# x by tokens on row halves of the array, a batch in one run

## The chip, the cores and the metric

The kernel runs on one core of a Trainium2 chip. The metric is the device time of one execution in microseconds; the median over three runs is 315.53 us (315.52 to 315.60).

## The reference, cut to what matters

```python
# attention without softmax: 8 batches, 8 heads, 576 tokens, head_dim 64
kv = einsum('bhsd,bhse->bhde', k, v)          # 64 x 64 for each head
o = einsum('bhsd,bhde->bhse', q, kv)
x = o / sqrt(mean(o * o, axis=-1) + 1e-6) * g_norm
# the heads side by side: x is 4608 tokens x 512
a = x @ w_a; b = x @ w_b                      # d_ff = 1536
out = (a * b) @ w_out                         # 4608 x 512
```

## The kernel before, in words

The matmuls run in bf16 with fp32 sums in PSUM, which is one tile `P` of 8 banks of 512 columns. The 4608 tokens are taken in 9 strips of 512 (`STRIP`). A strip of the feed-forward part has 12 units (`Unit`, one for each 128 columns of d_ff): group a is 4 matmuls with `w_a` as weights (`part_a`), which ScalarE casts into `asb` (L335); group b is 4 with `w_b` (`part_b`), which VectorE multiplies by `asb` into `ab` (L339). After the units come four groups of 12 matmuls with `w_out` (`ffn_o`, L156), each copied out by ScalarE or VectorE in turn and stored through the SP queue.

Batches 0 and 1 of the attention part are worked at the start, by head. Batches 2 to 7 are worked by token, one batch in each of the strips 1 to 6, in between the units: batch `b = s + 1` in strip `s`, whose x the next strips read from `xt`. The order is written out by hand: `slot(A, s, n)` is called after unit or output group n, and with n - 0.5 between its two halves, and it issues the piece that is due at that n.

A batch by token goes like this. `kv` forms k^T v of each pair of heads, as 40 matmuls on the two column halves of the array (L173), into bank 7; in strips 3 and 5 it is done for two batches. `kv_out` copies the results into `kvb`, one 128 x 128 block for each pair of heads, whose off-diagonal quarters are zero (L184). Then x comes in five chunks of 128 tokens (576 tokens: the fifth starts at 448 and uses only its last 64). For chunk c, `tx` runs 4 matmuls, one for each pair of heads, with 128 tokens of q^T as weights (128 rows: two heads of 64) and the block of `kvb` streamed (128 columns), into bank 5 + c % 3 (L271), and ScalarE squares it (L278). A half step later `tss` sums by head on VectorE (L282), another half later `trs` takes the reciprocal root on ScalarE (L287) and GpSimd multiplies it with g (L294), and 1.5 steps after that `txt` multiplies on VectorE (L303) and issues a DMA transpose into `xt` on the SP queue (L305).

The groups of the units take their banks from `ab_bank()`, which goes round 4, 1, 2, 0; output groups take bank 3 (`O`) or a bank of that round in turn. So banks 0 to 4 belong to the feed-forward part and 5 to 7 to the attention part.

```python
AB = (4, 1, 2, 0)
n_ab = [0]
def ab_bank():
    n_ab[0] += 1
    return AB[(n_ab[0] - 1) % len(AB)]
```

q, k and v of batches 2 to 7 are loaded by DMAs that GpSimd issues (`load_late`); it first waits, in a copy of one element (`gate`, L136), for an earlier q^T. `transpose_q` brings q^T by a DMA transpose on the SP queue.

Of the kernel before, what the change touches and what calls it, by code (L numbers as in the profile page):

```python
# [8 lines left out]
FP32 = mybir.dt.float32  # L9
BF16 = mybir.dt.bfloat16  # L10
AF = mybir.ActivationFunctionType
# [4 lines left out]
def kernel(  # L16
# [11 lines left out]
    nc = tc.nc  # L28

    B, H, S, D = q.shape  # L30
    d_model = H * D
# [4 lines left out]
    NP = H // 2  # L36
    HF = S // 2
    STRIP = 512
# [10 lines left out]
    def sb(shape, dt, name):  # L49
        return pool.tile(shape, dt, name=name, tag=name)  # L50
# [11 lines left out]
    LC = S // 128  # L62
# [4 lines left out]
    qT = [sb([128, NP, S], BF16, f"qT{i}") for i in range(2)]  # L67
    kvs = [sb([128, NP, D], BF16, f"kvs{i}") for i in range(2)]

    kvb = [sb([128, NP, 128], BF16, f"kvb{i}") for i in range(2)]  # L70
    xt = sb([128, KC, n_tok], BF16, "xt")
    abt = [[sb([128, STRIP], BF16, f"ab{i}_{f}") for f in range(FC)] for i in range(2)]
    a_sb = [sb([128, STRIP], BF16, f"asb{i}") for i in range(4)]
# [1 line left out]
    rs = [sb([128, 2, HF], FP32, f"rs{i}") for i in range(3)]  # L75

    k_x = sb([128, 2 * EC * D], FP32, "k_x")
    k32 = k_x[0:EP].rearrange("p (h c d) -> p h c d", h=2, c=EC)

    sqt = [sb([128, H, D], FP32, f"sqt{i}") for i in range(2)]  # L80
    sqt.append(k_x[:, 0 : H * D].rearrange("p (h d) -> p h d", h=H))
    sst = [sb([128, H], FP32, f"sst{i}") for i in range(3)]
    rst = [sb([128, H], FP32, f"rst{i}") for i in range(3)]
    g_all = sb([128, D], FP32, "g_all")
    o_sb = [sb([128, d_model], FP32, f"osb{i}") for i in range(4)]
    o_end = sb([128, d_model // 2], FP32, "o_end")
# [18 lines left out]
    P = psum.tile([128, 8, STRIP], FP32, name="P", tag="P")  # L105
    O = 3
# [47 lines left out]
    def product(o, lhsT, rhs, halves=False, **kw):  # L154
        for r in (slice(0, D), slice(D, 2 * D)) if halves else (slice(0, 2 * D),):
            nc.tensor.matmul(o[r], lhsT=lhsT[:, r], rhs=rhs, **kw)  # L156


    class Attn:
# [18 lines left out]
                        stop=(c == len(rows) - 1),  # L178
                    )

        def kv_out(self, ps, src, copy=nc.scalar.copy):
            for j in range(2):
                r = slice(j * D, (j + 1) * D)
                copy(kvb[self.b % 2][r, ps, r], src[r])  # L184


        def kv1(self, p, i):
# [60 lines left out]
        def x(self, p, i0, halves=False):  # L248
            for h in range(2):
                product(  # L250
                    P[:, i0 + h, 0:HF],
                    kvb[self.b % 2][:, p, :],
                    self.qT[:, p, h * HF : (h + 1) * HF],
                    halves,
                    start=True,
                    stop=True,
                )
# [4 lines left out]
            t0 = min(c * 128, S - 128)  # L262
            return t0, slice(c * 128 - t0, 128)

        def by_head(self, i):
            return P[:, i, :].rearrange("t (h d) -> t h d", h=H)

        def tx(self, c, i):
            t0, r = self.rows(c)
            for p in range(NP):  # L270
                nc.tensor.matmul(  # L271
                    P[:, i, p * 128 : (p + 1) * 128],
                    lhsT=self.qT[:, p, t0 : t0 + 128],
                    rhs=kvb[self.b % 2][:, p, :],
                    start=True,
                    stop=True,
                )
            nc.scalar.activation(sqt[c % 3][r], self.by_head(i)[r], AF.Square)  # L278

        def tss(self, c):  # L280
            _, r = self.rows(c)
            nc.vector.reduce_sum(sst[c % 3][r], sqt[c % 3][r], axis=mybir.AxisListType.X)  # L282

        def trs(self, c):
            _, r = self.rows(c)
            n = r.stop - r.start
            nc.scalar.activation(  # L287
                rst[c % 3][r],
                sst[c % 3][r],
                AF.Abs_reciprocal_sqrt,  # L290
                bias=eps_t[r],
                scale=1.0 / D,
            )
            nc.gpsimd.tensor_mul(  # L294
                sqt[c % 3][r],
                rst[c % 3][r].unsqueeze(2).to_broadcast([n, H, D]),
                g_all[r].unsqueeze(1).to_broadcast([n, H, D]),
            )

        def txt(self, c, i):  # L300
            t0, r = self.rows(c)
            t = x_tok[c // 3][:, c % 3]
            nc.vector.tensor_mul(t[r], self.by_head(i)[r], sqt[c % 3][r])  # L303
            t0 += self.b * S
            nc.sync.dma_start_transpose(  # L305
                xt[:, :, t0 + r.start : t0 + 128], t[r].rearrange("t h d -> t (h d)")
            )


    class Unit:  # L310
        n = 0
# [30 lines left out]
            self.part_a(kcs)  # L342
            self.part_b(kcs)

    AB = (4, 1, 2, 0)
    n_ab = [0]

    def ab_bank():
        n_ab[0] += 1
        return AB[(n_ab[0] - 1) % len(AB)]  # L350

    def ffn_ab(s, fc, between=None):
        u = Unit(s, fc, ab_bank(), ab_bank())
        u.part_a()
        if between:
            between()
        u.part_b()
# [69 lines left out]
    make_identity(nc, ident, nomemset=True)  # L427
    nc.scalar.activation(warm, eps_t, AF.Abs_reciprocal_sqrt)
    nc.vector.memset(ones, 0.0)
    for t in kvb:  # L430
        nc.vector.memset(t, 0.0)
    for t in ktl + vtl:
        nc.vector.memset(t[S - 128 * LC :, :, LC, :], 0.0)
    nc.vector.memset(ones[0:D, 0:D], 1.0 / D)
# [18 lines left out]
    A = Attn(0)  # L453
# [9 lines left out]
    t = P[:, 2, :].bitcast(BF16)[:, 0:S].rearrange("q (c t) -> q c t", c=EC)  # L463
# [4 lines left out]
    for c in range(EC):  # L468
        nc.tensor.matmul(
            P[:, SS, 0 : 2 * D],  # L470
            lhsT=kc0[:, c, :],
            rhs=vc[:, c, :],
            start=(c == 0),
            stop=(c == EC - 1),
        )
    for j in range(2):
        r = slice(j * D, (j + 1) * D)
# [7 lines left out]
    for p in range(1, NP):  # L485
        i = X[p % 2]
# [34 lines left out]
    u3.part_a()  # L521
    u2.part_b()
    u3.part_b()
    n_ab[0] = 0
    for fc in range(4, FC):
        ffn_ab(0, fc)

# [1 line left out]
    A = Attn(1)  # L529
# [27 lines left out]
    u1.first((0, 1, 2))  # L557
    u0.rest((3,))
    u1.rest((3,))
    n_ab[0] = 1  # L560


    def slot(A, s, n):

        kb = P[:, 7, :].rearrange("q (b p e) -> q b p e", b=2, e=D)
        if s == 1:
            k0, xs = 5, (6.5, 8, 9.5, 11, 12.5)
        else:
            k0, x0 = {2: (2, 3.5), 3: (4, 5.5), 4: (0, 1.5), 5: (4, 5.5), 6: (0, 1.5)}[s]
            xs = tuple(x0 + x for x in (0, 1.5, 2.5, 4, 5))  # L570

        if n == k0 and s in (1, 2, 3, 5):
            two = [A] if s < 3 else [A, Attn(s + 2)]
            for i, a in enumerate(two):
                for p in range(NP):
                    a.kv(p, kb[:, i, p, :])
            for i, a in enumerate(two):
                a.kv_out(slice(0, NP), kb[:, i], nc.vector.tensor_copy if i else nc.scalar.copy)
        for c, x in enumerate(xs):
            i = 5 + c % 3  # L580
            if n == x:
                A.tx(c, i)
            elif n == x + 0.5:
                A.tss(c)
            elif n == x + 1:
                A.trs(c)
            elif n == x + 2.5:
                A.txt(c, i)

    for s in range(1, N_STRIP - 1):  # L590
        b = s + 1
        A = Attn(b) if b < B else None
        for n in range(FC + 4):
            amid = (lambda n=n: slot(A, s, n - 0.5)) if A else None
            if n >= FC:
                ffn_o(s, n - FC, ab_bank() if n % 2 else O, amid)
            elif s > 1 or n > 1:
                ffn_ab(s, n, amid)
            if A:
                slot(A, s, n)  # L600

            if s == 1 and n == 3:
                load_late(3)
            if b + 1 < B and n == (12, 4, 8, 5, 8)[s - 1]:
                transpose_q(b + 1)
            if b + 2 < B and n == (14, 10, 14, 8)[s - 1]:
                load_late(b + 2)
# [43 lines left out]
```

## Time and profile before

| what | value |
|---|---|
| median of three runs | 315.53 us |
| the profiled execution's own time | 315.56 us |
| its span, first to last instruction | 313.8 us |
| TensorE's clock granted | 1.00 |
| TensorE busy | 308.6 us, 98% |
| VectorE, ScalarE, GpSimd busy | 141.5, 115.9, 101.2 us |
| matmuls of `tx` (L271) | 120 |
| matmuls of k^T v by token (L173) | 240 of 324 |

The profile is one execution. A matmul's row shows its length from its first to its last effect; matmuls overlap, so the distance of their starts, not the length, is what one costs in a stream. L numbers are lines of the kernel before. Times in the timeline are microseconds from the span's start.

### The profile page before, as it was taken

Reading aid. Unit: us, or ns where it says so; the run is one execution under the profiler, and the core shown is the slowest. Engines: PE = TensorE matmul, PEld = TensorE weight load, DVE = VectorE, ACT = ScalarE, POOL = GpSimd, SP = SyncE. Lnnn points to the kernel's source line nnn. Section 1 sums busy time; section 2 is a strip of 40 time slices with the busy share of each in tenths; the row PEclk is TensorE's granted clock in tenths of the full one; section 3 lists DMA queues with packets and bytes.
Section 4 is the critical chain, followed back from the end, with each engine's and each line's share of the span. In section 5 each row is a group of like instructions: output and inputs, shape, how many; then the busy total and the mean of one; then the engine's idle time right before and its main releaser. Section 6 shows DMA issues by size and latency. Waiting matters only on the chain.

```text
span 313.8 us, 5034 instructions
## 1 busy us (share of the span) xinstructions
PE 308.6 (98%) x1935; PEld 149.0 (47%) x1935; DVE 141.5 (45%) x235; ACT 115.9 (37%) x225; POOL 101.2 (32%) x123
## 2 busy tenths in 40 slices
PE   8999999999999999999999999999999999999995
PEld 3544474454445444544454445544544444444443
DVE  4544335356337703583377123761683134214321
ACT  3643155453246313551464024622651233123310
POOL 8954891282453730139038200320230000000000
PEclk9999999999999999999999999999999999999999
DMA  8999999999799799059988980073022200030002
GB/s 182 197 196 199 201 183 160 229 146 157 172 171 166 103 197 154 2 95 139 207 125 116 169 175 2 17 159 111 1 50 60 102 0 0 36 100 1 0 36 100
DMA packets 94253, 36.19 MB, mean 115 GB/s; under 512 B 64918, under 2 KB 89750, under 8 KB 94230
## 3 DMA queue, kind: packets, MB, share of 16 engines
q0 software_dynamic: 59120, 18.44, 53.8%
q1 hardware_dynamic: 34642, 16.87, 23.3%
q10 hardware_dynamic: 468, 0.57, 0.6%
q8 instruction: 15, 0.25, 0.3%
q14 instruction: 8, 0.07, 0.1%
HBM read 37.78 MB, written 12.98 MB: 162 GB/s over the span
## 4 chain that ended last, share of the span: by engine, by line
PE 86%; DMA 7%; POOL 4%; issue 1%; ACT 0%; POOLq 0%
PE P L321 53%; PE P L156 29%; DMA wb_t<-in_moe_w_b_dram 6%; PE P L271 2%; PE P L173 2%; DMA vt<-in_v_dram 2%; POOL qt L116 1%; POOL wo_t L131 1%; POOL kt L116 1%; POOL vt L116 1%; POOL wa_t L441 0%; POOL wb_t L441 0%; PE P L197 0%; POOL wa_t L127 0%; ACT o_end L619 0%
## 5 line engine op out<-in xcount | busy, mean ns | idle before, releaser
L339 DVE TENSOR_TENSOR ab<-P,asb 128x512 bf16<-128x512 f32 x108 | 74.5, 691 | 103.5 <-PE P L321 87.0
L321 PE MATMUL P<-xt,wa_t 128*128 128x512 bf16 x432 | 111.9, 380 | 0.0
L321 PE MATMUL P<-xt,wb_t 128*128 128x512 bf16 x432 | 111.8, 379 | 0.0
L335 ACT CAST asb<-P 128x512 bf16<-128x512 f32 x108 | 63.0, 585 | 92.4 <-PE P L321 92.4
L156 PE MATMUL P<-wo_t,ab 128*128 128x512 bf16 (+2 forms) x462 | 95.8, 374 | 0.0
L156 PEld LDWEIGHTS <-ab 128*128 128x128 bf16 (+1 forms) x462 | 43.7, 99 | 48.0
L321 PEld LDWEIGHTS <-wa_t 128*128 128x128 bf16 x432 | 41.4, 98 | 47.4 <-issue 0.2
L321 PEld LDWEIGHTS <-wb_t 128*128 128x128 bf16 x432 | 41.5, 98 | 47.0 <-DMA wb_t<-in_moe_w_b_dram 0.2
L294 POOL TENSOR_TENSOR sqt<-rst,g_all 128x512 f32<-128x512 f32 (+1 forms) x24 | 25.0, 1043 | 96.2 <-ACT rst L287 96.2
L392 ACT COPY osb<-P 128x512 f32<-128x512 f32 x17 | 9.9, 585 | 67.5 <-PE P L156 62.2
L394 DVE COPY osb<-P 128x512 f32<-128x512 f32 x18 | 12.4, 691 | 44.0 <-PE P L156 39.5
L139 POOL DMA_DIRECT2D qs<-in_q_dram x12 | 19.8, 1653 | 0.7 <-issue 0.3
L282 DVE TENSOR_REDUCE sst<-sqt 128x8 f32<-128x512 f32 (+1 forms) x24 | 16.3, 680 | 1.9 <-ACT sqt L278 1.4
L303 DVE TENSOR_TENSOR qv<-P,sqt 128x512 bf16<-128x512 f32 (+1 forms) x24 | 16.5, 686 | 0.3
L278 ACT ACTIVATE sqt<-P 128x512 f32<-128x512 f32 (+1 forms) x24 | 14.4, 599 | 4.2 <-PE P L271 4.1
L271 PEld LDWEIGHTS <-qT 128*128 128x128 bf16 x120 | 9.2, 98 | 7.1
L271 PE MATMUL P<-kvb,qT 128*128 128x128 bf16 x120 | 11.6, 220 | 0.0
L287 ACT ACTIVATE rst<-sst,eps_t 128x8 f32<-128x8 f32 (+1 forms) x30 | 9.0, 300 | 4.6 <-DVE sst L282 4.3
L238 DVE SCALAR_TENSOR_TENSOR xt<-P,g_col,rs 128x288 bf16<-128x288 f32 x16 | 7.5, 512 | 5.2 <-ACT rs L228 5.2
L294 POOL TENSOR_TENSOR k_x<-rst,g_all 128x512 f32<-128x512 f32 x6 | 6.3, 1042 | 8.8 <-ACT rst L287 8.8
L131 POOL DMA_DIRECT2D wo_t<-in_moe_w_out_dram x12 | 6.4, 530 | 6.7 <-DMA wb_t<-in_moe_w_b_dram 3.2
L184 ACT CAST kvb<-P 64x64 bf16<-64x64 f32 (+1 forms) x16 | 4.6, 285 | 10.5 <-PE P L173 10.4
(67 smaller groups left out, 123.1 us busy)
## 6 DMA issues: line engine op xcount, KB each, us to landing
out_dram<-osb SPq DMA_DIRECT2D x23, 256.0 KB, 2.1
qs<-in_q_dram POOLq DMA_DIRECT2D x12, 288.0 KB, 6.9
ktl<-in_k_dram POOLq DMA_DIRECT2D x6, 512.0 KB, 8.8
vtl<-in_v_dram POOLq DMA_DIRECT2D x6, 512.0 KB, 11.6
out_dram<-osb SPq DMA_DIRECT2D x13, 128.0 KB, 2.3
wo_t<-in_moe_w_out_dram POOLq DMA_DIRECT2D x12, 128.0 KB, 6.0
wa_t<-in_moe_w_a_dram POOLq DMA_DIRECT2D x5, 256.0 KB, 9.2
wb_t<-in_moe_w_b_dram POOLq DMA_DIRECT2D x5, 256.0 KB, 9.8
```

The source lines that it names most:

```text
L139: nc.gpsimd.dma_start(out=d[:, hs, :], in_=q[b, hs].rearrange("h t d -> t h d"))
L156: nc.tensor.matmul(o[r], lhsT=lhsT[:, r], rhs=rhs, **kw)
L271: nc.tensor.matmul(P[:, i, p * 128 : (p + 1) * 128], lhsT=self.qT[:, p, t0 : t0 + 128], rhs=kvb[self.b % 2][:, p, :], start=True, stop=True,)
L278: nc.scalar.activation(sqt[c % 3][r], self.by_head(i)[r], AF.Square)
L282: nc.vector.reduce_sum(sst[c % 3][r], sqt[c % 3][r], axis=mybir.AxisListType.X)
L294: nc.gpsimd.tensor_mul(sqt[c % 3][r], rst[c % 3][r].unsqueeze(2).to_broadcast([n, H, D]), g_all[r].unsqueeze(1).to_broadcast([n, H, D]),)
L303: nc.vector.tensor_mul(t[r], self.by_head(i)[r], sqt[c % 3][r])
L321: nc.tensor.matmul(self.a if w is wa_t else self.b, lhsT=w[:, kc, self.fc * 128 : (self.fc + 1) * 128], rhs=xt[:, kc, t0 : t0 + STRIP], st ...
L335: nc.scalar.copy(self.t, self.a)
L339: nc.vector.tensor_mul(abt[self.s % 2][self.fc], self.b, self.t)
L392: nc.scalar.copy(t, P[:, i, :])
L394: nc.vector.tensor_copy(t, P[:, i, :])
```

## The change

x of a batch is formed in one run, not five. Each pair's matmul of 128 rows becomes two of 64 rows, on the lower and the upper half of the array's rows: weights are 128 tokens of one head's q^T, and the 64 columns of that head's k^T v (`kvs`, without the zero quarters) are streamed. The two heads of a pair go to different banks. Chunks 0 and 1 share banks 4 and 6, chunks 2 and 3 banks 5 and 7; the last chunk goes into bank 3 (the outputs') and one bank that is taken out of the units' round at that place (`lent`), and ScalarE copies it at once into an SBUF tile (`x_last`, on the memory of `rs[0]`), from where its square and its product read it.

The units' round is 4, 1, 2, 0 in strip 0, as before, and 0, 1, 2 from strip 1 on. k^T v by token leaves PSUM in one copy for each batch into `kvs`, on VectorE for the first batch and on ScalarE for the second; before there were two copies into `kvb` for each. `kvb` is one buffer and not two; batch 1 alone still uses it. Squares are issued by `tsq`, 1.5 steps apart; sums follow at 1, 2, 4, 5 and 7 steps after the run, roots and products a half step later, `txt` a whole step after those. The run starts at the step where the first chunk was before in strips 1, 3 and 5, and one unit earlier in strips 2, 4 and 6; in strip 2 k^T v is one unit earlier too. The first lines of `slot` still set `xs`, which nothing reads then.

```diff
-    kvb = [sb([128, NP, 128], BF16, f"kvb{i}") for i in range(2)]
+    kvb = sb([128, NP, 128], BF16, "kvb")
...
+    x_last = rs[0].rearrange("t h s -> t (h s)")[:, 0:d_model]
+    x_last = x_last.rearrange("t (j p d) -> t j p d", j=2, p=NP)
...
-        def tx(self, c, i):
-            t0, r = self.rows(c)
-            for p in range(NP):
-                nc.tensor.matmul(
-                    P[:, i, p * 128 : (p + 1) * 128],
-                    lhsT=self.qT[:, p, t0 : t0 + 128],
-                    rhs=kvb[self.b % 2][:, p, :],
-                    start=True,
-                    stop=True,
-                )
-            nc.scalar.activation(sqt[c % 3][r], self.by_head(i)[r], AF.Square)
+        def place(self, c):
+            if c == LC:
+                return (self.lent, 0), (O, 0)
+            return tuple((4 + 2 * j + c // 2, c % 2 * (STRIP // 2)) for j in range(2))
...
+        def tx(self, lent):
+            self.lent = lent
+            for c in range(LC + 1):
+                t0, _ = self.rows(c)
+                for p in range(NP):
+                    for j, (i, c0) in enumerate(self.place(c)):
+                        r = slice(j * D, (j + 1) * D)
+                        nc.tensor.matmul(
+                            P[:, i, c0 + p * D : c0 + (p + 1) * D],
+                            lhsT=self.qT[r, p, t0 : t0 + 128],
+                            rhs=self.kvs[r, p, :],
+                            start=True,
+                            stop=True,
+                        )
+            _, r = self.rows(LC)
+            nc.scalar.copy(x_last[r], P[r, lent : O + 1 : O - lent, 0 : STRIP // 2])
+
+        def tsq(self, c):
+            _, r = self.rows(c)
+            nc.scalar.activation(sqt[c % 3][r], self.by_head(c)[r], AF.Square)
...
-    AB = (4, 1, 2, 0)
-    n_ab = [0]
+    ab_banks = [4, 1, 2, 0]
     def ab_bank():
-        n_ab[0] += 1
-        return AB[(n_ab[0] - 1) % len(AB)]
+        ab_banks.append(ab_banks.pop(0))
+        return ab_banks[-1]
...
-    n_ab[0] = 1
+    ab_banks[:] = [0, 1, 2]
...
     def slot(A, s, n):
...
+        k0, x0 = {1: (5, 6.5), 2: (1, 2.5), 3: (4, 5.5), 4: (0, 0.5), 5: (4, 5.5), 6: (0, 0.5)}[s]
...
-                a.kv_out(slice(0, NP), kb[:, i], nc.vector.tensor_copy if i else nc.scalar.copy)
-        for c, x in enumerate(xs):
-            i = 5 + c % 3
-            if n == x:
-                A.tx(c, i)
-            elif n == x + 0.5:
-                A.tss(c)
-            elif n == x + 1:
-                A.trs(c)
-            elif n == x + 2.5:
-                A.txt(c, i)
+                (nc.scalar.copy if i else nc.vector.tensor_copy)(a.kvs, kb[:, i])
+        m = n - x0
+        if m == 0:
+            A.tx(ab_bank())
+        for c in range(LC + 1):
+            if m == 1.5 * c:
+                A.tsq(c)
+            if m == (1, 2, 4, 5, 7)[c]:
+                A.tss(c)
+            if m == (1, 2, 4, 5, 7)[c] + 0.5:
+                A.trs(c)
+            if m == (1, 2, 4, 5, 7)[c] + 1.5:
+                A.txt(c)
```

More of the change, by code (lines that the diff above doesn't have):

```diff
@@ L78 @@
     k32 = k_x[0:EP].rearrange("p (h c d) -> p h c d", h=2, c=EC)
-    sqt = [sb([128, H, D], FP32, f"sqt{i}") for i in range(2)]
-    sqt.append(k_x[:, 0 : H * D].rearrange("p (h d) -> p h d", h=H))
+    sqt = [sb([128, 2, NP, D], FP32, f"sqt{i}") for i in range(2)]
+    sqt.append(k_x[:, 0 : H * D].rearrange("p (j h d) -> p j h d", j=2, h=NP))
     sst = [sb([128, H], FP32, f"sst{i}") for i in range(3)]
     rst = [sb([128, H], FP32, f"rst{i}") for i in range(3)]
+    x_last = rs[0].rearrange("t h s -> t (h s)")[:, 0:d_model]
+    x_last = x_last.rearrange("t (j p d) -> t j p d", j=2, p=NP)
     g_all = sb([128, D], FP32, "g_all")
@@ L179, in kv, with kv_out @@
                     )
-        def kv_out(self, ps, src, copy=nc.scalar.copy):
+        def kv_out(self, ps, src):
             for j in range(2):
                 r = slice(j * D, (j + 1) * D)
-                copy(kvb[self.b % 2][r, ps, r], src[r])
+                nc.scalar.copy(kvb[r, ps, r], src[r])
         def kv1(self, p, i):
@@ L251, in x @@
                     P[:, i0 + h, 0:HF],
-                    kvb[self.b % 2][:, p, :],
+                    kvb[:, p, :],
                     self.qT[:, p, h * HF : (h + 1) * HF],
@@ L263, in rows, with by_head @@
             return t0, slice(c * 128 - t0, 128)
-        def by_head(self, i):
-            return P[:, i, :].rearrange("t (h d) -> t h d", h=H)
-        def tx(self, c, i):
-            t0, r = self.rows(c)
-            for p in range(NP):
-                nc.tensor.matmul(
-                    P[:, i, p * 128 : (p + 1) * 128],
-                    lhsT=self.qT[:, p, t0 : t0 + 128],
-                    rhs=kvb[self.b % 2][:, p, :],
-                    start=True,
-                    stop=True,
-                )
-            nc.scalar.activation(sqt[c % 3][r], self.by_head(i)[r], AF.Square)
+        def place(self, c):
+            if c == LC:
+                return (self.lent, 0), (O, 0)
+            return tuple((4 + 2 * j + c // 2, c % 2 * (STRIP // 2)) for j in range(2))
+        def by_head(self, c):
+            if c == LC:
+                return x_last
+            (i, c0), (j, _) = self.place(c)
+            o = P[:, i : j + 1 : j - i, c0 : c0 + STRIP // 2]
+            return o.rearrange("t j (p d) -> t j p d", p=NP)
+        def tx(self, lent):
[17 more added lines that the diff above has]
+            nc.scalar.activation(sqt[c % 3][r], self.by_head(c)[r], AF.Square)
         def tss(self, c):
             _, r = self.rows(c)
-            nc.vector.reduce_sum(sst[c % 3][r], sqt[c % 3][r], axis=mybir.AxisListType.X)
+            nc.vector.reduce_sum(
+                sst[c % 3][r],
+                sqt[c % 3][r].rearrange("t j p d -> t (j p) d"),
+                axis=mybir.AxisListType.X,
+            )
         def trs(self, c):
@@ L294, in trs @@
             nc.gpsimd.tensor_mul(
-                sqt[c % 3][r],
+                sqt[c % 3][r].rearrange("t j p d -> t (j p) d"),
                 rst[c % 3][r].unsqueeze(2).to_broadcast([n, H, D]),
@@ L298, in trs, with txt @@
             )
-        def txt(self, c, i):
+        def txt(self, c):
             t0, r = self.rows(c)
             t = x_tok[c // 3][:, c % 3]
-            nc.vector.tensor_mul(t[r], self.by_head(i)[r], sqt[c % 3][r])
+            nc.vector.tensor_mul(
+                t[r].rearrange("t (p j) d -> t j p d", j=2), self.by_head(c)[r], sqt[c % 3][r]
+            )
             t0 += self.b * S
@@ L429 @@
     nc.vector.memset(ones, 0.0)
-    for t in kvb:
-        nc.vector.memset(t, 0.0)
+    nc.vector.memset(kvb, 0.0)
     for t in ktl + vtl:
@@ L523 @@
     u3.part_b()
-    n_ab[0] = 0
     for fc in range(4, FC):
```

## The prediction

> **What bounds the kernel now.** I read the shares of busy time first, then TensorE's own waits, then the windows by strip, then short stretches of the timeline.
>
> ```profile
> PE 308.6 (98%) x1935; PEld 149.0 (47%) x1935; DVE 141.5 (45%) x235; ACT 115.9 (37%) x225; POOL 101.2 (32%) x123
> PE P L321 53%; PE P L156 29%; DMA wb_t<-in_moe_w_b_dram 6%; PE P L271 2%; PE P L173 2%; DMA vt<-in_v_dram 2%; POOL qt L116 1%; POOL wo_t L131 1%; POOL kt L116 1%; POOL vt L116 1%; POOL wa_t L441 0%; POOL wb_t L441 0%; PE P L197 0%; POOL wa_t L127 0%; ACT o_end L619 0%
> ...
> PE P L407 <- DVE eps_t L424: 1.2, 1, 1.2
> PE P L156 <- ACT sq L220: 0.4, 1, 0.4
> ```
>
> The second line is the chain that ended last; the last two are all of TensorE's waits for other engines, both before 10 us. From 50 us on TensorE is never idle, so the end moves by what the change adds to TensorE's stream or takes from it, plus any wait that it makes for TensorE. The windows are cut where strips begin (columns: stretch, length, PE busy and count, and so on).
>
> ```profile
> 83.47:116.52 33.05, 33.05 (x205) 15.82 (x204) 15.92 (x24) 13.02 (x26) 18.42 (x19) 1.00 1.35 159
> 116.52:150.21 33.69, 33.69 (x246) 16.45 (x244) 16.85 (x26) 13.02 (x26) 11.79 (x12) 1.00 0.74 106
> 150.21:182.41 32.20, 32.20 (x166) 15.20 (x164) 15.91 (x24) 12.29 (x24) 11.79 (x12) 1.00 1.21 160
> 248.29:279.37 31.08, 31.08 (x146) 14.11 (x144) 9.69 (x14) 8.19 (x14) 0.00 (x0) 1.00 0.09 34
> ```
>
> The fourth strip is feed-forward work alone. The third adds the x of one batch (L271, 5 times 4 matmuls): 32.20 - 31.08 = 1.12 us, 56 ns for a weight load with its 128-column matmul. The first adds a k^T v of one batch too (L173, 40 matmuls by column halves): 33.05 - 32.20 = 0.85. The second has k^T v of two batches: 33.69 - 33.05 = 0.64 more for 20 more pairs, 32 ns a pair; the other 0.85 - 0.64 = 0.21 is paid once for each run. The timeline shows where:
>
> ```profile
> 59.96 0.81 PE L321 MATMUL P<-xt,wb_t 128*128 128x512 bf16 x3
> 60.70 0.82 PE L173 MATMUL P<-vtl,ktl 128*64 128x64 bf16 x40
> 61.46 0.61 PE L321 MATMUL P<-xt,wa_t 128*128 128x512 bf16 x2
> ```
>
> Full matmuls follow each other at 0.216 us (2.59 us for 12 in the chain), so the array was free at 59.96 + 3 x 0.216 = 60.61, but the halves start at 60.70, and the last of them starts 0.13 before the full array goes on.
>
> **What the Trainium skill says.** TensorEngine Tiling (Array Packing), section Key Properties: tiles run independently, and a change of tiling mode drains the array. The trace agrees: two matmuls of 64 columns in 32 ns, and 0.21 us for entering and leaving. Its section Gotcha 1: PSUM Pressure wants different row tiles in different banks; the change puts them so (4 with 6, 5 with 7, the lent bank with 3). TensorE: Matmul & The Clock Gate, section LDWEIGHTS, prices a load by its columns, P/1.2 ns, so 53 ns for 64 columns; the 32 ns pairs contradict that. Its section on weight-path perf modes says that loads of 128 non-fp32 columns take a fast path, about twice as quick, and the tiling page excludes column tiling from it. No run so far shows a load of 128 columns on 64 rows.
>
> **The change, part by part.**
>
> Removed: in each of six strips the five groups of L271, 1.12 us.
>
> Added: one run of 40 loads and 40 matmuls, 64 rows each, 64 columns streamed, in 20 pairs on the two row halves. The trace before has only L211 with row halves (64 x 64, 288 columns), whose two matmuls start 3 ns apart. So a run costs 0.21 + 20c, and the pair's time c is unknown. Lower bound: streaming 64 columns at 215.8 ns per 512 plus a few ns, 29. Upper bound with halves side by side: 56, the whole step of today, if the load of 128 columns and not the stream sets it. Upper bound of all: two such steps, 112. I take 32, from L173: there a slow 64-column load hides within 32 ns, and a load of twice the columns on a path twice as fast should hide as well. It supports this a little that six loads of 128 columns went by while the clock was still low (512 columns took 0.42 us there):
>
> ```profile
> 5.51 0.66 PE L465 MATMUL P<-ident,qc 96*128 96x96 bf16 x6
> 5.97 0.63 PE L407 MATMUL P<-zeros 128*128 128x512 bf16 x1
> ```
>
> (5.97 - 5.51) / 6 = 77 ns, no more than streaming 96 columns takes there, so the load is at most about 40 ns at the full clock, if it scales. The run is then 0.85 us.
>
> A new wait for TensorE: the units of the loop now turn over three banks, not four. In the unit where the run sits, its groups take banks X and Y, the run's last chunk Z, and the next unit X and Y again. Its second group wants Y only one group (0.86 us) after the last one wrote Y. The release is read here:
>
> ```profile
> 63.20 1.03 PE L321 MATMUL P<-xt,wa_t 128*128 128x512 bf16 x4
> 63.47 0.69 DVE L339 TENSOR_TENSOR ab<-P,asb 128x512 bf16<-128x512 f32 x1 [1.89 <-PE P L321]
> ...
> 64.06 0.39 PE L271 MATMUL P<-kvb,qT 128*128 128x128 bf16 x4
> 64.28 0.59 PE L321 MATMUL P<-xt,wb_t 128*128 128x512 bf16 x2
> ...
> 8.66 0.65 ACT L220 ACTIVATE sq<-P 128x576 bf16<-128x576 f32 x1 [1.90 <-PE P L211]
> 9.36 0.41 PE L156 MATMUL P<-sq,ones 128*128 128x288 bf16 x2 [0.43 <-ACT sq L220]
> ```
>
> The multiply starts 0.27 after the next group begins, takes 0.69, and TensorE follows a release by 9.36 - 9.31 = 0.05: 1.01 - 0.86 = 0.15 us of waiting, once in each strip. Bounds: 0, if VectorE starts sooner; 0.5, if a piece of x is still ahead of the multiply there (none is in program order). Everything on TensorE is queued behind it. In other units two groups (1.73 us) lie between, 0.72 to spare; where txt (0.69) and tss (0.68) stand between two multiplies, these come 2.06 apart, not 1.73, and 0.4 remains.
>
> At nothing: the copy of the last chunk on ScalarE (64 x 512, about 0.59 as L278 in that shape). After the run ScalarE does it and a square (0.60), 1.2 us, and the next cast is due only 1.73 us after the run. The copy frees the lent bank and bank 3; the former is wanted 2.6 us on, the latter at the strip's end. Squares and txt over two banks and a reordered output keep their element counts. k^T v leaves by one copy, not two (L184 has 0.37 each); the run comes 2.6 us later. The one memset fewer is beside the first DMAs. In strips 2, 4 and 6 the run stands one unit earlier: strip 2's would be at 90.4, and the gate's copy read its q^T at 84.1. The loads for batch 5, behind GpSimd's last product, go one half unit (0.86) later: they landed at 123.45, are used at 125.8, and 1.5 us stay. On SP strip 2's first xt transpose now stands behind q's, which holds the queue to 99.6; xt is needed at 116.5. No DMA is added.
>
> Sum for each strip: -1.12 + 0.85 + 0.15 = -0.12 us; six strips, **-0.7 us**. The profiled execution took 315.56 (span 313.8 and 1.8 around it), 0.03 from the median of 315.53, so the same difference is taken from either: 314.8.
>
> **Rivals.** About 0.2% (0.63 us) can be told from no change. The balance is at 0.21 + 20c + 0.15 = 1.12, c = 38 ns; under 33 it is faster by over 0.2%, over 43 slower.
>
> Loads bind (slower): the two 128-column loads of a pair set its time, as today's step might be set. At c = 56 it is 6 x (0.21 + 1.12 + 0.15 - 1.12) = +2.2, 317.7. For it: the loads double in number while the stream under each halves. Against: 32 ns for pairs of slower loads.
>
> Halves don't run side by side, so the change does not do what it says: 40 steps of 29 to 56 ns, +2.4 to +8.9, 318 to 324. Against: L211's starts 3 ns apart.
>
> Balance: c between 33 and 43, the gain eaten by loads and the bank wait, 314.9 to 316.1.
>
> More gain: c = 29 gives -1.1, 314.4; without the bank wait too, -2.0.
>
> A bank or a DMA late elsewhere: three banks with 0.4 us to spare; 0.2 in three units of each strip would be 3.6 us, 318.4.
>
> **Numbers.** Side by side at 29 to 33: 0.50, of which 0.44 over the bound and 0.06 within; balance 0.15; loads bind 0.22; one after the other 0.08; another wait 0.05. Faster 0.44, same 0.21, slower 0.35. The range runs from 314.2 (c = 29 and a shorter bank wait) to 317.7 (loads bind); for the likeliest case alone it is 314.2 to 315.2.
>
> **What would show it.** Right: the matmuls of tx in 20 pairs about 32 ns apart, a run of 0.85 us in the chain, TensorE waiting six times about 0.15 us for the multiply that is L339 now, and the last strip at 31.08 still. Wrong: pairs at over 43 ns, starts evenly spaced, waits of TensorE elsewhere, or a strip without a run that is longer.

## The result and the profile after

The changed kernel takes 316.61 us (median of six runs) against 315.53 for the kernel before in the same comparison: the ratio is 1.0033, with a 95% interval of 1.0020 to 1.0046. It is slower by about 1.1 us. The forecast was 314.8 us, 0.7 faster. Line numbers from here on are those of the changed kernel: `tx` is L292, the copy of the last chunk L302, the units' matmuls L355, casts L369 and multiplies L373.

TensorE still has nearly all of the span, but its list of waits has grown. The first line gives the engines' busy time; the others are TensorE's own waits (us in total, times, longest; lines left out are marked).

```profile
PE 304.8 (97%) x2020; PEld 145.5 (46%) x2055; DVE 140.3 (45%) x234; ACT 116.5 (37%) x225; POOL 101.2 (32%) x123
...
PE P L355 <- ACT rs L302: 2.0, 3, 0.7
PE P L440 <- DVE eps_t L457: 1.2, 1, 1.2
...
PE P L355 <- DVE ab L373: 0.4, 2, 0.2
```

`rs` in the first wait is the memory of `x_last`: three times TensorE waited for ScalarE's copy of the last chunk. The third wait is the foreseen one, at the units' banks. It shows twice in this list and six times in the starts of the matmuls: a matmul's row is 0.38 us long, longer than the 0.216 us between starts, so a stop of 0.15 us stays under the row of the matmul before and shows as idle time only where that row is missing from the trace.

The windows, cut where the strips begin, say in which strips it happened.

```profile
50.50:84.11 33.61, 32.73 (x222) 15.32 (x224) 17.08 (x27) 13.10 (x26) 11.78 (x12) 1.00 1.29 162
84.11:116.99 32.88, 32.67 (x221) 15.29 (x224) 16.23 (x25) 12.76 (x25) 18.42 (x19) 1.00 1.36 164
116.99:150.51 33.52, 33.31 (x262) 15.88 (x264) 16.23 (x25) 13.13 (x26) 8.20 (x8) 1.00 0.57 106
150.51:183.26 32.75, 31.71 (x182) 14.70 (x184) 15.80 (x24) 12.79 (x25) 15.38 (x17) 1.00 1.40 159
183.26:216.78 33.52, 33.31 (x262) 15.92 (x264) 16.23 (x25) 13.12 (x26) 5.21 (x5) 1.00 0.38 81
216.78:249.53 32.75, 31.72 (x181) 14.69 (x184) 15.81 (x24) 12.79 (x25) 5.21 (x5) 1.00 0.21 57
249.53:280.61 31.08, 30.92 (x142) 14.11 (x144) 9.68 (x14) 8.19 (x14) 0.00 (x0) 1.00 0.09 35
```

These are strips 1 to 7. The prediction shows strips 2, 3, 4 and 7 of the kernel before; its strips 1, 5 and 6 are these:

```profile
50.41:83.47 33.06, 33.06 (x206) 15.82 (x204) 16.86 (x26) 13.29 (x27) 11.80 (x12) 1.00 1.30 172
182.41:216.10 33.69, 33.69 (x245) 16.46 (x244) 16.85 (x26) 13.01 (x26) 5.20 (x5) 1.00 0.36 81
216.10:248.29 32.19, 32.19 (x165) 15.19 (x164) 15.82 (x24) 12.38 (x24) 5.21 (x5) 1.00 0.20 56
```

Read only the second column, the strip's length. Strips 2, 3 and 5 got shorter by 0.17 us each (32.88 for 33.05, 33.52 for 33.69 twice). Strips 1, 4 and 6 got longer by about 0.55 (33.61 for 33.06, 32.75 for 32.20 and for 32.19). Strip 7 is 31.08 as before. Together that is 3 x 0.55 - 3 x 0.17 = 1.14 us; strip 1 begins 0.09 later (50.50 for 50.41), and the spans differ by 1.2 (315.0 and 313.8). So nothing to speak of is left over.

The timeline of strip 4 shows the extra stretch (in brackets, the engine's idle time before the row and who ended it).

```profile
153.03 0.76 PE L292 MATMUL P<-kvs,qT 64*128 64x64 bf16 x40
153.19 0.58 ACT L369 CAST asb<-P 128x512 bf16<-128x512 f32 x1 [1.20 <-PE P L355]
...
153.83 0.58 ACT L302 COPY rs<-P 64x512 f32<-64x512 f32 x1
154.44 0.60 ACT L306 ACTIVATE sqt<-P 128x512 f32<-128x512 f32 x1
154.46 1.02 PE L355 MATMUL P<-xt,wb_t 128*128 128x512 bf16 x4 [0.67 <-ACT rs L302]
```

The row of the run ends at 153.79. Group b of the same unit (L355) needs nothing from that run, yet it starts at 154.46, when ScalarE's copy has ended (153.83 + 0.58 = 154.41). In strip 2 the same group does not wait:

```profile
90.94 0.76 PE L292 MATMUL P<-kvs,qT 64*128 64x64 bf16 x40
...
91.64 1.04 PE L355 MATMUL P<-xt,wb_t 128*128 128x512 bf16 x3
91.75 0.58 ACT L302 COPY rs<-P 64x512 f32<-64x512 f32 x1
```

Here group b begins at 91.64, before the copy has even started. From the start of the run to group b it is 154.46 - 153.03 = 1.43 us in strip 4 and 91.64 - 90.94 = 0.70 in strip 2. The starts of the single matmuls put the difference at 0.74 us in all six strips: 0.83 from the end of the last pair to group b in strips 1, 4 and 6, and 0.09 in strips 2, 3 and 5.

### The profile page after: what moved, and what is told of

Same layout as the page of the kernel before. It is cut to its first block, busy times and chain, and to the rows that moved or that the text cites. A ratio compares the mean times of both kernels' runs of the same rounds, so it can differ in the third digit from the quotient of the medians.

```text
span 315.0 us, 5222 instructions
## 1 busy us (share of the span) xinstructions
PE 304.8 (97%) x2020; PEld 145.5 (46%) x2055; DVE 140.3 (45%) x234; ACT 116.5 (37%) x225; POOL 101.2 (32%) x123
## 4 chain that ended last, share of the span: by engine, by line
PE 94%; DMA 2%; ACT 1%; issue 1%; DVE 0%; ACTq 0%; DVEq 0%
PE P L355 59%; PE P L159 31%; PE P L176 2%; DMA qv<-in_v_dram 2%; PE P L292 1%; PE P L200 1%; ACT rs L302 1%; PE P L214 0%; DVE ab L373 0%; ACT sq L223 0%; PE P L440 0%; ACT vc L493 0%; PE P L501 0%; ACTq L449 0%; ACT o_end L653 0%
## 5 line engine op out<-in xcount | busy, mean ns | idle before, releaser
L373 DVE TENSOR_TENSOR ab<-P,asb 128x512 bf16<-128x512 f32 x108 | 74.4, 691 | 106.4 <-PE P L355 104.3
L355 PE MATMUL P<-xt,wb_t 128*128 128x512 bf16 x424 | 110.9, 379 | 2.8 <-ACT rs L302 2.0
L355 PE MATMUL P<-xt,wa_t 128*128 128x512 bf16 x416 | 110.2, 379 | 0.8 <-issue 0.2
L369 ACT CAST asb<-P 128x512 bf16<-128x512 f32 x108 | 62.9, 585 | 93.4 <-PE P L355 93.4
L355 PEld LDWEIGHTS <-wb_t 128*128 128x128 bf16 x432 | 41.9, 98 | 52.9 <-issue 3.6
L355 PEld LDWEIGHTS <-wa_t 128*128 128x128 bf16 x432 | 41.8, 98 | 49.9 <-issue 0.2
L335 DVE TENSOR_TENSOR qv<-P,sqt 128x512 bf16<-128x512 f32 x18 | 12.2, 680 | 0.0
L306 ACT ACTIVATE sqt<-P 128x512 f32<-128x512 f32 x18 | 10.5, 584 | 0.1
L231 ACT ACTIVATE rs<-P,eps_t 128x576 f32<-128x576 f32 (+1 forms) x9 | 6.1, 687 | 3.8 <-PE P L159 3.5
L440 PE MATMUL P<-zeros 128*128 128x512 bf16 x16 | 6.2, 538 | 1.2 <-DVE eps_t L457 1.2
L139 POOL COPY gate<-qT 1x1 bf16<-1x1 bf16 x5 | 0.9, 176 | 17.4 <-DMA qT<-qs 17.2
```

Of the source, the lines that this page charges most:

```text
L306: nc.scalar.activation(sqt[c % 3][r], self.by_head(c)[r], AF.Square)
L335: nc.vector.tensor_mul(t[r].rearrange("t (p j) d -> t j p d", j=2), self.by_head(c)[r], sqt[c % 3][r])
L355: nc.tensor.matmul(self.a if w is wa_t else self.b, lhsT=w[:, kc, self.fc * 128 : (self.fc + 1) * 128], rhs=xt[:, kc, t0 : t0 + STRIP], st ...
L369: nc.scalar.copy(self.t, self.a)
L373: nc.vector.tensor_mul(abt[self.s % 2][self.fc], self.b, self.t)
```

## The experiments

What differs between the two kinds of strips is in the banks. The copy reads `P[r, lent : O + 1 : O - lent, ...]`, a stepped slice over two banks, the lent one and bank 3. The round of 0, 1, 2 lends bank 0 in strips 1, 4 and 6, where group b has bank 2, and bank 1 in strips 2, 3 and 5, where group b has bank 0. **Theory A**: the slice is ordered in the built program as a range from the lent bank to bank 3, so a group in a bank between the two stands behind the copy, although the copy does not read that bank. **Rival B**: ScalarE is late in strips 1, 4 and 6, by their place or by what it has to do there. **Rival C**: the row-halved run itself leaves the array late.

### Two copies of one bank each

```diff
-            nc.scalar.copy(x_last[r], P[r, lent : O + 1 : O - lent, 0 : STRIP // 2])
+            for j, i in enumerate((lent, O)):
+                nc.scalar.copy(x_last[r, j], P[r, i, 0 : STRIP // 2].rearrange("t (p d) -> t p d", p=NP))
```

> The last chunk leaves PSUM in two copies of one bank each, not in one copy with a stepped slice over the lent bank and bank 3. Theory A (the stepped slice is ordered as if it covered the banks between, so a group b in bank 2 has to stand behind it where bank 0 is lent): the three waits of 0.74 us go, 316.6 - 2.2 = 314.4 us, 0.3% under the kernel before. Rival B (in strips 1, 4 and 6 ScalarE is late, and the group would wait for it anyway): two copies are longer than one, 316.6 to 317.5. Rival C (the row-halved run itself leaves the array late): 316.6.

Measured: 314.65 us, ratio to the kernel before 0.9966 (0.9954 to 0.9978). The waits for the copy are gone; this is all that the list has, and none of it comes after 10 us:

```profile
PE P L441 <- DVE eps_t L458: 1.2, 1, 1.2
PE P L159 <- ACT sq L223: 0.4, 1, 0.4
PE P L498 <- DVE qc L491: 0.3, 1, 0.3
PE P L502 <- DVE qT L207: 0.2, 1, 0.2
```

(The six stops of 0.15 us at the units' banks are still in the starts of the matmuls, under the rows before them.) ScalarE does more than before and TensorE waits less, which speaks against B. It does not yet tell whether the banks or the form of the copy did it.

### The banks alone, both ways

```diff
-    ab_banks[:] = [0, 1, 2]
+    ab_banks[:] = [1, 2, 0]      # first kernel: group b below the lent bank everywhere
+    ab_banks[:] = [1, 0, 2]      # second kernel: group b between it and bank 3 everywhere
```

> Only the order of the three banks in the round is changed, 1, 2, 0 in place of 0, 1, 2: the run is lent bank 2 in strips 2, 3 and 5 and bank 1 in the others, and the group b after it then stands in bank 1 or 0, under the lent one. Instructions, places and sizes stay. Theory A: no wait for the copy in any strip, 314.4 us. Rivals B and C: the waits follow the strips and not the banks, 316.6.

> The same with the order 1, 0, 2: bank 0 is lent in strips 2, 3 and 5 with group b in bank 1, and bank 1 in the others with group b in bank 2, always one that lies between the lent one and bank 3. Theory A: six waits of 0.74 us in place of three, 316.6 + 2.2 = 318.8 us. Rivals B and C: 316.6.

Measured: 314.48 us, 0.9970 (0.9959 to 0.9981), and 318.75 us, 1.0100 (1.0087 to 1.0113). The instructions, their places and their sizes are the same as in the changed kernel; only bank numbers differ. In the list of TensorE's waits the first kernel has none for the copy. For the second, the first line has six times where the changed kernel had three:

```profile
PE P L355 <- ACT rs L302: 4.0, 6, 0.7
```

So the wait goes with the banks and with nothing else of a strip: 318.75 - 316.61 = 2.1 us for three more, 316.61 - 314.48 = 2.1 for three fewer, 0.7 each. A holds, B and C fall. The built programs say the same directly. The first matmul of group b carries a wait for ScalarE. In strips 1, 4 and 6 of the changed kernel it waits for the copy L302, which reads banks 0 and 3, though the group writes bank 2. In strips 2, 3 and 5 it waits for an earlier cast (L369) that read the group's own bank. With two copies, and with group b below the lent bank, it is such a cast in all six strips; with group b between the two banks it is the copy in all six. So the order is put in when the program is built. That no data pass between the copy and the group is plain from the code.

### The next unit takes the lent bank

The two copies stay, and the round is turned after the run:

```diff
             A.tx(ab_bank())
+            ab_banks[1], ab_banks[2] = ab_banks[2], ab_banks[1]
```

> Two copies as in e1, and the two banks that follow in the round after the run change places, so that group b of the next unit takes the lent bank and not the one whose multiply has just begun. If the 0.15 us in each strip is the reuse of that bank after one group: six of them go, 314.4 - 0.9 = 313.5 us, 0.6% under the kernel before, and TensorE waits for nothing after 50 us. If the multiply was late for another reason, or the copy holds the lent bank past 1.7 us: 314.4 or more.

Measured: 313.53 us, 0.9935 (0.9922 to 0.9948). The foreseen 0.15 us in each strip was real and goes away with the early reuse of the bank: 314.65 - 313.53 = 1.1, against 0.9 worked out. The starts have 0.15 six times with the two copies and none here, so 0.9; the other 0.2 is within the spread of the runs (313.44 to 313.85). It is the fastest kernel here that forms all of x, 0.65% under the kernel before.

### The row halves undone

From the last kernel, the run is put back to whole rows, and with it what they need: `kvb` in two buffers with two copies for each batch, and the last chunk in one bank with one copy. Cut to the matmuls:

```diff
-                    for j, (i, c0) in enumerate(self.place(c)):
-                        r = slice(j * D, (j + 1) * D)
-                        nc.tensor.matmul(
-                            P[:, i, c0 + p * D : c0 + (p + 1) * D],
-                            lhsT=self.qT[r, p, t0 : t0 + 128],
-                            rhs=self.kvs[r, p, :],
+                    nc.tensor.matmul(
+                        P[:, 4 + c if c < LC else lent, p * 128 : (p + 1) * 128],
+                        lhsT=self.qT[:, p, t0 : t0 + 128],
+                        rhs=kvb[self.b % 2][:, p, :],
```

> e4 with the row halves alone undone: one run of 20 matmuls of 128 rows and 128 columns from kvb (two buffers and two copies again), chunks 0 to 3 in banks 4 to 7, the last chunk in the lent bank alone and copied out in one copy of 64 x 512. If the row halves themselves are the gain: 20 x 0.056 = 1.12 us for a run in place of 0.80, six times 0.32, 313.5 + 1.9 = 315.4 us, as the kernel before. If the gain came from having one run in one place, or from the lighter evacuations: 313.5.

Measured: 315.39 us, 1.0000 (0.9991 to 1.0008). With whole rows, one run in one place is worth nothing. Since the copies out of PSUM went back too, the time alone does not tell them from the row halves; the length of the run does. The chains of strip 2, with row halves (the fastest kernel) and with whole rows (this one), have these lines for the run (start, length):

```profile
90.25 0.69 PE P L292 x40
```

```profile
90.27 1.12 PE P L289 x20
```

The first leaves out about 0.1 for entering the halves, so it is 0.79 against 1.12 us. Six times 0.33 is 2.0 us, the whole gain of the kernel it was made from; nothing is left for the copies.

### The run in two pieces

From the kernel in which the next unit takes the lent bank, the run is cut in two (the diff shows the calls alone):

```diff
         if m == 0:
             A.tx(ab_bank())          # chunks 0 and 1
...
+        if m == 0.5:
+            A.tx(None)               # chunks 2, 3 and the last, and the copies
```

> e4 with the run cut in two: chunks 0 and 1 where the run is, chunks 2, 3 and the last after the unit's group b. The number of matmuls stays. If entering and leaving the row halves costs 0.19 us each time: six more, 313.5 + 1.15 = 314.7 us. If the cost lies in the matmuls and not in the switch: 313.5.

Measured: 314.73 us, 0.9981 (0.9973 to 0.9989). One more entry and exit costs (314.73 - 313.53) / 6 = 0.20 us; the starts of the matmuls give 0.21. That is why the run has to be in one piece. By estimate, five groups in five places would pay 0.2 five times, 1.0 us, and the halves save only 1.12 - 20 x 0.029 = 0.54 in the stream.

### Half the stream

From the same kernel; half of x is left out:

```diff
-                            P[:, i, c0 + p * D : c0 + (p + 1) * D],
+                            P[:, i, c0 + p * D : c0 + p * D + D // 2],
...
-                            rhs=self.kvs[r, p, :],
+                            rhs=self.kvs[r, p, 0 : D // 2],
```

> e4 with 32 columns streamed by each matmul of the run and not 64 (half of x is left out; the same loads, instructions and banks; one memset of unwritten columns in strip 0). If the stream sets the 29 ns of a pair: 16 ns, 120 pairs less 13 ns, 313.5 - 1.6 = 311.9 us. If the loads of 128 columns set it, as the prediction's rival has it: 313.5. In between: the loads are the bound somewhere between 16 and 29 ns.

Measured: 312.85 us, 0.9914 (0.9901 to 0.9928), between the two. By its chain a run is 0.60 us, with 0.69 in the kernel it was made from:

```profile
90.09 0.60 PE P L292 x40
```

By the starts of the matmuls a pair takes 25 ns and not 29. So two loads of 128 columns need no more than 25 ns, and at 64 columns they are not what sets the pair's 29 ns; the stream, by estimate 64 x 215.8 / 512 = 27 ns, accounts for nearly all of it. With 32 columns the stream would be 13 ns, so there something else than the stream holds the pair at 25: the loads or the issue of the instructions. Which of the two it is stays open.

## Why the prediction was wrong

**What bounds the kernel**: right. The end moved by what TensorE's stream and its waits gained and lost, strip by strip.

**The time of a pair, c**: the likeliest case held, on the good side. It was taken as 32 ns and is 29, the lower bound that the prediction gave; the run is 0.80 us, not 0.85 (by the starts 0.10 to enter, 0.69 up to group b, 0.01 more behind group b's first matmul). The two halves of a pair start 3 to 4 ns apart. So the rival of binding loads and the rival of halves one after the other are refuted, as strips 2, 3 and 5 also say, which got shorter. Six strips at c = 29 alone would have been -1.1 us.

**The wait for the reused bank**: right in place, size and number, 0.15 us in each strip. Strips 2, 3 and 5 show the sum of both, -1.12 + 0.80 + 0.15 = -0.17, as measured.

**The step that failed** is the line "At nothing: the copy of the last chunk on ScalarE". It priced the copy by ScalarE's time and by the two banks that the copy frees. Both were right: TensorE waited for no cast there, and neither bank was wanted early. It never asked who else is ordered behind the copy. The slice is written over a range of banks, and the group b that follows it in TensorE's queue lies in that range in three of six strips. TensorE stands still there for 0.20 us from the last pair to the start of the copy, 0.58 for the copy and 0.05 for the release: 0.83 in place of 0.09, a cost of 0.74 that the sum put at nothing. Without it the changed kernel would take 314.5 us (the kernel with group b below the lent bank everywhere measures it), within 0.3 us of the forecast; 3 x 0.7 us lie between a gain and a loss. The rival that spoke of a bank late elsewhere looked at slack between reuses, which was enough, and so missed it. Of the signs of being wrong, one came: a wait of TensorE elsewhere.

That 316.61 us lies inside the range given, 314.2 to 317.7, is luck: the upper part of the range was there for loads that bind, and they did not.

**The cover for the rest** held: the casts, squares, sums, the GpSimd products and the queues on SP cost TensorE nothing in strips 2, 3 and 5, and the last strip is still 31.08 us.

## What to carry to other kernels

When a copy reads two separated banks in one stepped slice, look at which instructions write into the banks between them just after it, since they may be ordered behind it; here two copies of one bank each, or an order of banks that leaves nothing between, took the wait away. Row halves pay when a zero-padded block is streamed, but only in a run long enough to carry one entry and one exit: here 20 pairs saved 0.54 us against 0.2. When banks are lent out of a round, work through the next unit's banks by hand: here the lent bank was the better one for it.

## What the runs showed that was not expected

Two matmuls of 64 rows and 64 columns, each with its own load of 128 columns, follow the pair before them by 29 ns, where a pair on column halves with loads of half as many columns takes 32. With 32 columns streamed a pair still takes 25 ns. Entering and leaving the row halves cost as much as for column halves, about 0.2 us together.
